# Attention with a gated layer on one core: the weights' conversion moved into PSUM, one stock of PSUM banks, and a new instruction order

## The chip, the cores and the metric

The kernel runs on one core of a Trainium2 chip. The metric is the device time of one execution, in microseconds (us). Engines are named as in the profile: PE is TensorE's matmul stream and PEld its weight loads, DVE is VectorE, ACT is ScalarE, POOL is GpSimd, SP issues the DMAs.

## The reference

There are 4 batches with 8 heads each, 1152 keys of width 64, and queries pooled in pairs to 576. Every head is softmax attention; the heads of a batch together give 576 tokens of width 512, which go through a gated layer with 1536 inner columns. The three weight matrices arrive as float64.

```python
def _attn_ref(q, k, v):
    q_pool = q.reshape(B, H, S // 2, 2, D).mean(axis=3)
    scores = np.matmul(q_pool, k.transpose(0, 1, 3, 2)) / np.sqrt(D)
    attn = np.exp(scores - np.max(scores, axis=-1, keepdims=True))
    attn = attn / (np.sum(attn, axis=-1, keepdims=True) + 1e-09)
    return np.matmul(attn, v)
def _moe_ref(x, w_gate, w_val, w_out):
    gate = 1.0 / (1.0 + np.exp(-(x @ w_gate)))
    return gate * (x @ w_val) @ w_out
```

## The kernel before, in words

The order of all instructions comes from a planner (`Plan`). Every step of the work is an `Op` with an engine, an assumed duration and a priority (a place in a sequence of heads, 18 places a head), and with the buffers that it takes and uses. `Plan.run` plays the steps through with the assumed durations and so fixes, once, the order in which each engine's instructions stand. On the chip each engine works through its own row strictly in that order and waits by semaphores; a step that comes late holds back everything behind it on its engine.

[...] The 32 heads are numbered u = 0 to 31, batch after batch:

- `head_operands` prepares a head. POOL adds the query pairs (L316). ACT writes the high halves of queries and keys (L321, L336); POOL writes their low halves (L339 for the keys, two pieces of 576 columns; L326 for some of the queries, else on DVE).
- `maxima` finds the largest score of each query: PE multiplies (L372, 384 columns), DVE reduces from PSUM (L377, L387, L389). The negated maxima are put on a diagonal in QB (L355 on POOL or DVE, L410 on POOL), so that the score product subtracts them.
- `half` does one half (288 queries) of a head: the score product into a PSUM bank (L469, two matmuls), the exponential on ACT. For the first 8 heads (`WHOLE`) one exponential and one product with the values (L486). For the others a rounded exponential eh (L473), a full one in place (L501), the difference el on DVE (L504), two products (L511, L515) and sums of eh on POOL (L533), which ACT and DVE split (L573, L576) for a last product (L580). `normalise` divides (L598 to L621).
- `convert` makes the weights usable. There are 36 pieces of 128x512 values. A piece is loaded as pairs of 32-bit words into cr (L632); ACT scales both words (L637, L642); DVE joins sign, high and low word, in place in cr (L646 `sign`, L651 `join`); ACT writes the high part (L655) and POOL the low part (L658) into cs; SP stores cs to a scratch array in DRAM (L662). The 36 pieces are spread over heads 3 to 16.
- `gated` runs the gated layer of a batch, interleaved with the attention of the next batch: 12 matmuls into one bank (L697), then ACT, DVE and POOL work (L740, L746, L750, L754), output products added up by L780 and L782. The layer of the last batch comes after all attention.

PSUM has eight banks. Before the change the planner holds them as two stocks: "b" with six for scores, value products, and gated products; "n" with two for the maxima alone:

```python
        "b": [bank[:, 512 * i:512 * i + 512] for i in range(SLOTS["b"])],
        "n": [bank[:, 512 * i:512 * i + 512] for i in range(SLOTS["b"], 8)],
```

Of the kernel before, what the change touches and what calls it, by code (L numbers as in the profile page):

```python
# [158 lines left out]
def attention_glu_kernel(ctx: ExitStack, tc: tile.TileContext, qT, kT, vt_in, v, wg, wv, wo, out):  # L159
    nc = tc.nc  # L160
    B, H, D = 4, 8, 64
    SK, SQ = 1152, 576
# [8 lines left out]
    SLOTS = {  # L171
# [3 lines left out]
    }  # L175
    pl = Plan(SLOTS, ("b", "n"))

# [25 lines left out]
    def change_first():  # L203
# [16 lines left out]
        "b": [bank[:, 512 * i:512 * i + 512] for i in range(SLOTS["b"])],  # L220
        "n": [bank[:, 512 * i:512 * i + 512] for i in range(SLOTS["b"], 8)],

# [35 lines left out]
    def tl(h):  # L258
        return TL[h.tag][h.slot]
# [8 lines left out]
    def act(n):  # L268
        return 0.01 + 0.975e-3 * n

    def dve(n):
        return 0.08 + 0.99e-3 * n

    def pool(n, two=True):
        return 0.14 + 2.2e-3 * n if two else 0.2 + 0.9e-3 * n

    def dma(kb):
        return 0.15 + kb / 250
# [14 lines left out]
    def head_operands(u, need):  # L293
# [39 lines left out]
        for k, s in enumerate((slice(0, SQ), slice(SQ, SK))):  # L333

            def k_hi(s=s):
                nc.scalar.activation(out=tl(kh)[0][:, s], in_=tl(kr)[:, s], func=ACTF.Copy)  # L336

            def k_lo(s=s):
                nc.gpsimd.tensor_tensor(out=tl(kh)[1][HI, s], in0=tl(kr)[HI, s], in1=tl(kh)[0][HI, s].bitcast(F32),  # L339
                                        op=ALU.subtract)  # L340

            a = pl.op("ACT", act(SQ), k_hi, at + 0.1 * k, after=[lk], uses=[kr] + ([kh] if k else []),
                      take=[] if k else [kh])
            ka.append(a)
            kb.append(pl.op("POOL", pool(SQ), k_lo, at + 6 + 0.1 * k, after=[a], uses=[kr, kh]))
        max_in, rest, hi_k, hi_q = [ql] + ka, [qb] + kb, ka, [qa, qb]
# [12 lines left out]
        if DGP(u):  # L359
            dg = pl.op("POOL", 2 * pool(256), lambda: diag(nc.gpsimd), need - 6, after=[am], uses=[pm, qh])  # L360
        else:
            dg = pl.op("DVE", 1.3, lambda: diag(nc.vector), need - 6, after=[am], uses=[pm, qh])
        return dict(k=kh, q=qh, v=vr, lv=lv, got=[dg] + max_in + rest, hi_k=hi_k, hi_q=hi_q)

    def maxima(at, pm, nt, lhs, rhs, out, after, uses):
        red = []
        for t in range(nt):
            for j in range(3):
                m = pl.hold("n")

# [10 lines left out]
                red.append(pl.op("DVE", dve(384), rmax, pr, after=[a], uses=[m] + ([pm] if red else []),  # L381
                                 take=[] if red else [pm], keep=KEEP))
# [65 lines left out]
    def half(u, g, st, hd, stat, vdep, pair, tk):  # L448
# [13 lines left out]
        for c in range(NC):  # L462
# [9 lines left out]
            def ex_hi(m=m, eh=eh):  # L472
# [3 lines left out]
                      uses=[hd["k"], hd["q"]], take=[m, eh])  # L476
            high = pl.op("ACT", act(GN), ex_hi, pos - 2, after=[o], uses=[m, eh])
            first = last is None
# [26 lines left out]

            o = pl.op("ACT", act(GN), ex, pos - 2, after=[high], uses=[m])
            exs.append(o)
# [32 lines left out]
        y, r = st["y"], st["r"]  # L540
        if whole:

            def cp():
                nc.scalar.activation(out=tl(y)[mine, a:b], in_=tl(av[0])[LO, 0:GN], func=ACTF.Copy)

            def cp2():
                nc.scalar.activation(out=tl(r)[mine, a:b], in_=tl(av[0])[HI, 0:GN], func=ACTF.Copy, bias=1e-9)

            ended.append(last)
            st["yo"][g].append(pl.op("ACT", act(GN), cp, at, after=[last], uses=[av[0], y]))  # L550
            st["yo"][g].append(pl.op("ACT", act(GN), cp2, at, after=[last], uses=[av[0], r]))
            return
# [74 lines left out]
    def convert(kind, m, s, due):  # L627
        src = {"wg": (wg, wv)[s], "wo": wo}[kind][m]
        cr, cs = pl.hold("cr"), pl.hold("cs")

# [37 lines left out]
        a = pl.op("DVE", 1.0, sign, due, after=[a, a0], uses=[cr])
        a = pl.op("DVE", 1.0, join, due, after=[a], uses=[cr])
        a = pl.op("ACT", act(512), hi, due, after=[a], uses=[cr], take=[cs])  # L670
        a = pl.op("POOL", pool(512), lo, due, after=[a], uses=[cr, cs])
        return pl.op("SP", dma(512), store, due, after=[a], uses=[cs], late=3.0)

# [203 lines left out]
```

## Time and profile before

| | us |
|---|---|
| median of 3 runs (964.74 to 965.56) | 965.55 |
| the profiled execution's own time | 966.0 |
| its span in the profile | 963.6 |

The profile gives for each engine the time in which an instruction of it was under way. An instruction counts from its start to its end, and on PE, ACT and DVE the next one can start before the last one has ended, so the sum of a group's durations is larger than its share of the busy time. "Idle before" is the time in which an engine had nothing under way before an instruction, with the instruction that ended the wait. Line numbers in the profile are those of the kernel before.

### The profile page before, as it was taken

To read this page: it belongs to the slowest core of one execution; us is meant where nothing else is said; L and a number is where in the kernel's file an instruction comes from. 1 tells how busy PE (TensorE), PEld (TensorE's weight loads), DVE (VectorE), ACT (ScalarE), POOL (GpSimd) and SP (SyncE) were. 2 spreads that over 40 slices of the span, in tenths; PEclk is the share of its full clock that TensorE was granted. 3 is DMA by queue.
4 is the path that set the end of the run, shared out by engine and by line. 5 is a ranking of instruction groups with operands and counts; after the bars stand their busy time and mean duration, and the time that the engine had idled before them with its cause. 6 is when DMAs were issued, how large, how long until landed. Compare 5 with 4: busy or idle time off the path is not lost.

```text
span 963.6 us, 18573 instructions
## 1 busy us (share of the span) xinstructions
PE 921.8 (96%) x6312; PEld 878.2 (91%) x6312; DVE 667.6 (69%) x1414; ACT 662.9 (69%) x1701; POOL 731.7 (76%) x796
## 2 busy tenths in 40 slices
PE   5989999999999999999999999999999999999998
PEld 3878877989998989889999999999999999999998
DVE  6576778878797998977778787877878786610112
ACT  4779788878887878677777778767777767522211
POOL 7586686988999989999988979979988967621211
PEclk9999999999999999999999999999999999999999
DMA  8687986765685848665554634544544433534532
GB/s 188 175 239 222 243 263 176 220 182 200 194 281 168 254 171 256 201 200 169 150 150 121 178 101 137 177 134 151 168 132 135 136 101 111 175 126 165 184 122 71
DMA packets 57566, 166.87 MB, mean 173 GB/s; under 512 B 17536, under 2 KB 21632, under 8 KB 51328
## 3 DMA queue, kind: packets, MB, share of 16 engines
q1 hardware_dynamic: 57472, 165.70, 56.7%
q8 instruction: 49, 0.80, 0.3%
q14 instruction: 45, 0.37, 0.1%
HBM read 132.12 MB, written 23.59 MB: 162 GB/s over the span
## 4 chain that ended last, share of the span: by engine, by line
PE 67%; POOL 10%; DVE 9%; ACT 8%; issue 3%; DMA 2%; POOLq 0%; DVEq 0%; ACTq 0%
PE bank L697 36%; PE bank L469 12%; PE bank L372 6%; PE bank L486 6%; POOL acc L533 5%; PE bank L515 4%; PE bank L511 4%; DVE cr L651 2%; DVE el L504 2%; ACT eh L473 2%; DVE pm L377 2%; ACT bank L501 1%; POOL cs L658 1%; DVE cr L646 1%; PE bank L580 1%
## 5 line engine op out<-in xcount | busy, mean ns | idle before, releaser
L697 PE MATMUL bank<-x,wg 128*128 128x288 f32 x2304 | 358.6, 296 | 2.2 <-ACT sg L740 1.1
L697 PEld LDWEIGHTS bank<-x,wg 128*128 128x128 f32 x2304 | 328.4, 188 | 4.3 <-DVE el L504 2.1
L533 POOL TENSOR_TENSOR acc<-acc,eh 128x288 f32<-128x288 f32 x312 | 261.4, 838 | 29.4 <-ACT eh L473 13.0
L504 DVE TENSOR_TENSOR el<-bank,eh 128x288 fp32r<-128x288 f32 x432 | 193.0, 452 | 86.0 <-ACT bank L501 81.6
L377 DVE TENSOR_REDUCE pm<-bank 128x1 f32<-128x384 f32 x384 | 206.6, 549 | 60.5 <-PE bank L372 58.4
L473 ACT ACTIVATE eh<-bank 128x288 fp32r<-128x288 f32 x432 | 175.9, 407 | 74.9 <-PE bank L469 69.4
L469 PE MATMUL bank<-QA,KA 128*128 128x288 f32 x576 | 172.7, 304 | 9.6 <-DVE el L504 3.2
L469 PE MATMUL bank<-QB,KB 128*128 128x288 f32 x576 | 169.1, 298 | 8.1 <-POOL QB L410 4.4
L501 ACT ACTIVATE bank<-bank 128x288 f32<-128x288 f32 x432 | 176.7, 409 | 0.1
L754 POOL TENSOR_TENSOR g<-sg,g 128x288 fp32r<-128x288 f32 x96 | 79.6, 829 | 104.6 <-ACT g L750 103.2
L372 PE MATMUL bank<-KA,QA 128*128 128x384 f32 x384 | 139.4, 377 | 12.1 <-ACT KA L336 8.5
L697 PE MATMUL bank<-g,wo 128*128 128x288 f32 x864 | 137.5, 295 | 1.0 <-ACT sg L740 0.8
L511 PE MATMUL bank<-eh,vt 128*128 128x288 f32 x432 | 128.3, 297 | 2.2 <-ACT eh L473 1.3
L515 PE MATMUL bank<-el,vt 128*128 128x288 f32 x432 | 128.6, 298 | 1.8 <-DVE el L504 1.5
L697 PEld LDWEIGHTS bank<-g,wo 128*128 128x128 f32 x864 | 124.3, 188 | 1.6 <-ACT sg L740 1.1
L469 PEld LDWEIGHTS bank<-QA,KA 128*128 128x128 f32 x576 | 109.1, 189 | 16.1 <-DVE el L504 5.4
L469 PEld LDWEIGHTS bank<-QB,KB 128*128 128x128 f32 x576 | 109.1, 189 | 10.2 <-POOL QB L410 5.5
L339 POOL TENSOR_TENSOR KB<-kr,KA 64x576 fp32r<-64x576 f32 x64 | 95.3, 1496 | 12.5 <-ACT KA L336 8.6
L746 DVE SCALAR_TENSOR_TENSOR sg<-sg,bank 128x288 f32<-128x288 f32 x96 | 43.1, 449 | 79.1 <-PE bank L697 77.6
L372 PEld LDWEIGHTS bank<-KA,QA 128*128 128x128 f32 x384 | 73.6, 192 | 25.4 <-DVE pm L377 9.6
L515 PEld LDWEIGHTS bank<-el,vt 128*128 128x128 f32 x432 | 81.5, 189 | 4.2 <-DVE el L504 3.0
L511 PEld LDWEIGHTS bank<-eh,vt 128*128 128x128 f32 x432 | 81.3, 188 | 3.7 <-ACT eh L473 2.6
(66 smaller groups left out, 1274.5 us busy)
## 6 DMA issues: line engine op xcount, KB each, us to landing
wg<-wg_d SPq DMA_DIRECT2D x48, 1024.0 KB, 5.1
kr<-in_kT_dram SPq DMA_DIRECT2D x64, 288.0 KB, 5.0
wo<-wo_d SPq DMA_DIRECT2D x36, 512.0 KB, 3.8
wg_d<-cs SPq DMA_DIRECT2D x24, 512.0 KB, 4.9
qr<-in_qT_dram SPq DMA_DIRECT2D x32, 288.0 KB, 4.0
KP<-KA SPq DMA_DIRECT2D x32, 288.0 KB, 4.1
vr<-in_v_dram SPq DMA_DIRECT2D x24, 288.0 KB, 3.0
cr<-in_wg_dram SPq DMA_DIRECT2D x12, 512.0 KB, 5.0
```

Of the source, the lines that this page charges most:

```text
L339: nc.gpsimd.tensor_tensor(out=tl(kh)[1][HI, s], in0=tl(kr)[HI, s], in1=tl(kh)[0][HI, s].bitcast(F32), op=ALU.subtract)
L372: nc.tensor.matmul(out=tl(m)[:, 0:384], lhsT=lhs(t), rhs=rhs()[:, j * 384:(j + 1) * 384], start=True, stop=True)
L377: nc.vector.tensor_reduce(out=o, in_=tl(m)[:, 0:384], axis=AXX, op=ALU.max)
L469: nc.tensor.matmul(out=tl(m)[:, 0:GN], lhsT=tl(hd["k"])[k][:, ks], rhs=tl(hd["q"])[k][:, a:b], start=(k == 0), stop=(k == 1))
L473: nc.scalar.activation(out=tl(eh), in_=tl(m)[:, 0:GN], func=ACTF.Exp, scale=1.0 / 16.0)
L501: nc.scalar.activation(out=p, in_=p, func=ACTF.Exp, scale=1.0 / 16.0)
L504: nc.vector.tensor_tensor(out=tl(el), in0=tl(m)[:, 0:GN], in1=tl(eh).bitcast(F32), op=ALU.subtract)
L511: nc.tensor.matmul(out=tl(av[0])[:, 0:GN], lhsT=pair(c, w), rhs=tl(eh), start=(c == 0), stop=(c == NC - 1))
L515: nc.tensor.matmul(out=tl(av[1])[:, 0:GN], lhsT=pair(c, 1 - w), rhs=tl(el), start=(c == 0), stop=(c == NC - 1 and not mine_c))
L533: nc.gpsimd.tensor_tensor(out=tl(acc), in0=tl(e0).bitcast(F32) if two else tl(acc), in1=tl(e1).bitcast(F32), op=ALU.add)
L697: nc.tensor.matmul(out=ps[:, 0:GN], lhsT=l, rhs=r, start=(n == 0 and j == 0), stop=(n == 3 and j == 2))
L754: nc.gpsimd.tensor_tensor(out=g[:, 1, a:b], in0=tl(sg), in1=g[:, 0, a:b].bitcast(F32), op=ALU.subtract)
```

## The change

The float64 words are no longer joined in place in SBUF. A piece now takes a PSUM bank (`wd`): ACT writes the scaled low word there, DVE's `sign` and `join` read the high word from cr and read and write the bank, ACT reads the high part from the bank, and the low part is formed by DVE instead of POOL. The two stocks of banks become one of eight, from which maxima, scores, products and conversions all take. From head 16 on, the second of the two low-half pieces of the keys is on DVE instead of POOL. The planner's assumed durations change, and with them the whole order. The count of PE instructions stays.

```diff
-        "b": 6, "n": 2, "K": 3, "Q": 3, "kr": 1, ...
+        "b": 8, "K": 3, "Q": 3, "kr": 1, ...
...
-        return 0.01 + 0.975e-3 * n
+        return 0.05 + 0.93e-3 * n
...
-        return 0.08 + 0.99e-3 * n
+        return 0.09 + 1.08e-3 * n
...
-    KEEP = 0.25
+    KEEP = 0.15
...
+    KLD = lambda u: u >= 16
...
-            def k_lo(s=s):
-                nc.gpsimd.tensor_tensor(out=tl(kh)[1][HI, s], in0=tl(kr)[HI, s], in1=tl(kh)[0][HI, s].bitcast(F32),
-                                        op=ALU.subtract)
+            by = "DVE" if k and KLD(u) else "POOL"
+
+            def k_lo(s=s, by=by):
+                e = nc.vector if by == "DVE" else nc.gpsimd
+                e.tensor_tensor(out=tl(kh)[1][HI, s], in0=tl(kr)[HI, s], in1=tl(kh)[0][HI, s].bitcast(F32),
+                                op=ALU.subtract)
...
-                m = pl.hold("n")
+                m = pl.hold("b")
...
-        cr, cs = pl.hold("cr"), pl.hold("cs")
+        cr, cs, wd = pl.hold("cr"), pl.hold("cs"), pl.hold("b")
+
+        def word():
+            return tl(wd)[:, 0:512].bitcast(U32)
...
-            low = tl(cr)[:, :, 0]
-
-            nc.scalar.activation(out=low, in_=low, func=ACTF.Copy, scale=2.0 ** -29, bias=-0.49)
+            nc.scalar.activation(out=word(), in_=tl(cr)[:, :, 0], func=ACTF.Copy, scale=2.0 ** -29, bias=-0.49)
...
-            nc.vector.scalar_tensor_tensor(out=low, in0=high, scalar=0x80000000, in1=low,
+            nc.vector.scalar_tensor_tensor(out=word(), in0=tl(cr)[:, :, 1], scalar=0x80000000, in1=word(),
...
-            nc.vector.scalar_tensor_tensor(out=low, in0=high, scalar=3, in1=low,
+            nc.vector.scalar_tensor_tensor(out=word(), in0=tl(cr)[:, :, 1], scalar=3, in1=word(),
...
-            nc.scalar.activation(out=tl(cs)[:, 0], in_=tl(cr)[:, :, 0].bitcast(F32), func=ACTF.Copy)
+            nc.scalar.activation(out=tl(cs)[:, 0], in_=tl(wd)[:, 0:512], func=ACTF.Copy)
...
-            nc.gpsimd.tensor_tensor(out=tl(cs)[:, 1], in0=tl(cr)[:, :, 0].bitcast(F32),
-                                    in1=tl(cs)[:, 0].bitcast(F32), op=ALU.subtract)
+            nc.vector.tensor_tensor(out=tl(cs)[:, 1], in0=tl(wd)[:, 0:512], in1=tl(cs)[:, 0].bitcast(F32),
+                                    op=ALU.subtract)
```

The following excerpts are the order of the built programs. In the changed file the same statements stand two to three lines lower (L649 is `sign`, L653 `join`, L660 `lo`, L507 el, L380 the maxima's reduction, L413 the small diagonal, L472 the score product).

VectorE, around the conversions at heads 9 and 10, before:

```order
L377 TENSOR_REDUCE pm_116<-bank 128x1
L576 TENSOR_TENSOR dh_104<-acc_102,dh_104 128x288
L646 SCALAR_TENSOR_TENSOR cr_142<-cr_142 128x512
L651 SCALAR_TENSOR_TENSOR cr_142<-cr_142 128x512
L504 TENSOR_TENSOR el_98<-bank,eh_94 128x288
L559 TENSOR_TENSOR y_122<-bank,t_106 64x288
```

and in the changed program:

```order
L649 SCALAR_TENSOR_TENSOR bank<-cr_141,bank 128x512
L507 TENSOR_TENSOR el_100<-bank,eh_92 128x288
L507 TENSOR_TENSOR el_101<-bank,eh_93 128x288
L562 TENSOR_TENSOR y_122<-bank,t_107 64x288
L579 TENSOR_TENSOR dh_105<-acc_103,dh_105 128x288
L507 TENSOR_TENSOR el_98<-bank,eh_94 128x288
L380 TENSOR_REDUCE pm_116<-bank 128x1
L565 TENSOR_TENSOR y_122<-bank,y_122 64x288
L507 TENSOR_TENSOR el_99<-bank,eh_95 128x288
```

The two instructions of a piece stood behind each other and behind L576; now they are apart, with el and reductions between them. The `join` of this piece follows 15 instructions after its `sign`, and its `lo` 6 after that; the piece holds its bank from ACT's write before the first of them to the last.

GpSimd, in front of the small diagonal of heads 2 and 3, before:

```order
L607 TENSOR_TENSOR y_122<-y_122,r_124 128x288
L658 TENSOR_TENSOR cs_144<-cr_143,cs_144 128x512
L621 TENSOR_TENSOR x_127<-y_122,x_127 128x288
L316 TENSOR_TENSOR qr_86<-qr_86 64x576
L658 TENSOR_TENSOR cs_145<-cr_141,cs_145 128x512
L410 TENSOR_TENSOR QB_84<-ident,pp_119 64x64
```

and in the changed program:

```order
L610 TENSOR_TENSOR y_122<-y_122,r_124 128x288
L413 TENSOR_TENSOR QB_84<-ident,pp_119 64x64
L413 TENSOR_TENSOR QB_82<-ident,pp_119 64x64
L624 TENSOR_TENSOR x_127<-y_122,x_127 128x288
L316 TENSOR_TENSOR qr_86<-qr_86 64x576
```

The two conversions are gone from POOL, and the diagonal stands ahead of the two other steps.

TensorE at the very start, before:

```order
L372 MATMUL bank<-KA_73,QA_79 128x384 x12
L469 MATMUL bank<-QA_79,KA_73 128x288
L469 MATMUL bank<-QB_82,KB_76 128x288
L372 MATMUL bank<-KA_74,QA_80 128x384 x2
L469 MATMUL bank<-QA_79,KA_73 128x288
```

and in the changed program:

```order
L375 MATMUL bank<-KA_73,QA_79 128x384 x12
L472 MATMUL bank<-QA_79,KA_73 128x288
L472 MATMUL bank<-QB_82,KB_76 128x288
L472 MATMUL bank<-QA_79,KA_73 128x288
L472 MATMUL bank<-QB_82,KB_76 128x288
```

The 12 products for the first maxima still come first, but now into eight banks instead of two, and the first scores follow without the next head's maxima between them.

## Rows read from the trace of the kernel before

**Rows 1.** The profile's page, head line.

```profile
span 963.6 us, 18573 instructions
```

**Rows 2.** Busy time by stretch: length, PE, PEld, DVE, ACT, POOL (instructions), PE clock, DMA share, GB/s.

```profile
40.00:160.00 120.00, 114.11 (x601) 97.08 (x599) 85.71 (x158) 98.19 (x237) 84.01 (x75) 1.00 0.84 234
160.00:430.00 270.00, 253.72 (x1756) 240.67 (x1755) 227.28 (x464) 216.06 (x554) 248.25 (x256) 0.99 0.66 207
430.00:840.00 410.00, 405.55 (x2951) 399.55 (x2951) 310.48 (x700) 304.14 (x816) 352.63 (x411) 1.00 0.47 143
...
350.00:400.00 50.00, 45.70 (x320) 43.16 (x320) 44.55 (x84) 39.42 (x102) 47.78 (x50) 1.00 0.70 219
```

**Rows 3.** Chain that ended last, in order of time: start, length, what (its last long piece).

```profile
839.83 120.67 PE bank L697 x909
```

**Rows 4.** Groups of 160 to 430 us on PE: count, busy and mean, idle before and releasers.

```profile
L372 PE MATMUL bank<-KA,QA 128*128 128x384 f32 x110 | 37.3, 345 | 1.6 <-DVE QA L326 1.1 <-DVE pm L377 0.4
L372 PE MATMUL bank<-KP,QP 128*128 128x384 f32 x15 | 5.5, 366 | 0.2 <-DVE pm L377 0.2
...
L469 PEld LDWEIGHTS bank<-QA,KA 128*128 128x128 f32 x162 | 30.6, 189 | 10.7 <-DVE sg L746 3.6 <-DVE el L504 3.0 <-ACT sg L740 1.8
```

**Rows 5.** Timeline near 200 us: start, length, engine, instruction, [idle before and releaser].

```profile
198.60 1.43 POOL L339 TENSOR_TENSOR KB<-kr,KA 64x576 fp32r<-64x576 f32 x1
...
199.44 0.90 DVE L576 TENSOR_TENSOR dh<-acc,dh 128x288 fp32r<-128x288 f32 x1
...
200.11 1.40 POOL L658 TENSOR_TENSOR cs<-cr,cs 128x512 fp32r<-128x512 f32 x1
...
200.27 1.79 DVE L646 SCALAR_TENSOR_TENSOR cr<-cr 128x512 uint32<-128x512 uint32 x1
...
202.09 1.17 DVE L651 SCALAR_TENSOR_TENSOR cr<-cr 128x512 uint32<-128x512 uint32 x1
...
203.18 0.44 DVE L504 TENSOR_TENSOR el<-bank,eh 128x288 fp32r<-128x288 f32 x1
...
203.68 0.40 PE L469 MATMUL bank<-QA,KA 128*128 128x288 f32 x1 [1.40 <-DVE el L504]
```

**Rows 6.** Groups of 160 to 430 us on DVE.

```profile
L504 DVE TENSOR_TENSOR el<-bank,eh 128x288 fp32r<-128x288 f32 x162 | 72.2, 450 | 24.6 <-ACT bank L501 23.8
L377 DVE TENSOR_REDUCE pm<-bank 128x1 f32<-128x384 f32 x109 | 59.0, 546 | 2.6 <-PE bank L372 2.1
L651 DVE SCALAR_TENSOR_TENSOR cr<-cr 128x512 uint32<-128x512 uint32 x20 | 24.5, 1225 | 0.2
L646 DVE SCALAR_TENSOR_TENSOR cr<-cr 128x512 uint32<-128x512 uint32 x20 | 20.6, 1031 | 1.4 <-ACT cr L637 1.4
...
L326 DVE TENSOR_TENSOR QA<-qr,QA 64x576 fp32r<-64x576 f32 x3 | 3.9, 1310 | 0.2
```

**Rows 7.** Timeline at 237 us: one of the short `sign` instructions.

```profile
236.84 0.67 DVE L646 SCALAR_TENSOR_TENSOR cr<-cr 128x512 uint32<-128x512 uint32 x1
```

**Rows 8.** Groups of 160 to 430 us on POOL: the conversions' low parts and the keys' low halves.

```profile
L339 POOL TENSOR_TENSOR KB<-kr,KA 64x576 fp32r<-64x576 f32 x18 | 28.9, 1611 | 1.2
L658 POOL TENSOR_TENSOR cs<-cr,cs 128x512 fp32r<-128x512 f32 x21 | 28.8, 1371 | 1.1 <-ACT cs L655 0.7
```

**Rows 9.** Timeline from 62 to 68 us: POOL, and the PE instruction that waited for it.

```profile
62.18 1.75 POOL L658 TENSOR_TENSOR cs<-cr,cs 128x512 fp32r<-128x512 f32 x1
...
66.00 1.28 POOL L658 TENSOR_TENSOR cs<-cr,cs 128x512 fp32r<-128x512 f32 x1
67.25 0.65 POOL L410 TENSOR_TENSOR QB<-ident,pp 64x64 fp32r<-64x64 f32 x2
...
67.59 0.40 PE L469 MATMUL bank<-QB,KB 128*128 128x288 f32 x1 [2.34 <-POOL QB L410]
```

**Rows 10.** Groups of 40 to 160 us on PE: the second matmul of the score products.

```profile
L469 PE MATMUL bank<-QB,KB 128*128 128x288 f32 x126 | 35.5, 299 | 5.4 <-POOL QB L410 4.4 <-POOL QB L355 1.0
```

**Rows 11.** Timeline of the start: a pair of reductions, the first diagonal, the first full score product.

```profile
14.62 1.13 DVE L377 TENSOR_REDUCE pm<-bank 128x1 f32<-128x384 f32 x2 [0.21 <-PE bank L372]
...
17.32 1.97 DVE L355 TENSOR_TENSOR QB<-ident,pm 64x256 fp32r<-64x256 f32 x2
...
19.44 0.58 PE L469 MATMUL bank<-QB,KB 128*128 128x288 f32 x1 [2.71 <-DVE QB L355]
```

More of the change, by code (lines that the diff above doesn't have):

```diff
@@ L175, in attention_glu_kernel @@
     }
-    pl = Plan(SLOTS, ("b", "n"))
+    pl = Plan(SLOTS, ("b",))
     const = ctx.enter_context(tc.tile_pool(name="const", bufs=1))
@@ L220, in attention_glu_kernel @@
         "b": [bank[:, 512 * i:512 * i + 512] for i in range(SLOTS["b"])],
-        "n": [bank[:, 512 * i:512 * i + 512] for i in range(SLOTS["b"], 8)],
         "K": list(zip(SK_T("KA"), SK_T("KB"))),
@@ L344, in head_operands @@
             ka.append(a)
-            kb.append(pl.op("POOL", pool(SQ), k_lo, at + 6 + 0.1 * k, after=[a], uses=[kr, kh]))
+            kb.append(pl.op(by, pool(SQ) if by == "POOL" else 1.0, k_lo, at + 6 + 0.1 * k, after=[a], uses=[kr, kh]))
         max_in, rest, hi_k, hi_q = [ql] + ka, [qb] + kb, ka, [qa, qb]
@@ L359, in head_operands @@
         if DGP(u):
-            dg = pl.op("POOL", 2 * pool(256), lambda: diag(nc.gpsimd), need - 6, after=[am], uses=[pm, qh])
+            dg = pl.op("POOL", 1.5, lambda: diag(nc.gpsimd), need - 6, after=[am], uses=[pm, qh])
         else:
@@ L380, in maxima @@
                 a = pl.op("PE", pe(384), mm, pr, after=after, uses=uses, take=[m])
-                red.append(pl.op("DVE", dve(384), rmax, pr, after=[a], uses=[m] + ([pm] if red else []),
+                red.append(pl.op("DVE", 0.49, rmax, pr, after=[a], uses=[m] + ([pm] if red else []),
                                  take=[] if red else [pm], keep=KEEP))
@@ L476, in half @@
                       uses=[hd["k"], hd["q"]], take=[m, eh])
-            high = pl.op("ACT", act(GN), ex_hi, pos - 2, after=[o], uses=[m, eh])
+            high = pl.op("ACT", 0.3, ex_hi, pos - 2, after=[o], uses=[m, eh])
             first = last is None
@@ L504, in lo @@
                 nc.vector.tensor_tensor(out=tl(el), in0=tl(m)[:, 0:GN], in1=tl(eh).bitcast(F32), op=ALU.subtract)
-            o = pl.op("ACT", act(GN), ex, pos - 2, after=[high], uses=[m])
+            o = pl.op("ACT", 0.345, ex, pos - 2, after=[high], uses=[m])
             exs.append(o)
@@ L536, in half @@
                     two = len(adds) == 2
-                    added = pl.op("POOL", pool(GN), add, pos + 0.5, after=[high, added, adds[0][1]],
+                    added = pl.op("POOL", 0.88, add, pos + 0.5, after=[high, added, adds[0][1]],
                                   uses=[eh] + ([adds[0][0]] if two else [acc]), take=[acc] if two else [])
@@ L550, in half @@
             st["yo"][g].append(pl.op("ACT", act(GN), cp, at, after=[last], uses=[av[0], y]))
-            st["yo"][g].append(pl.op("ACT", act(GN), cp2, at, after=[last], uses=[av[0], r]))
+            st["yo"][g].append(pl.op("ACT", 0.42, cp2, at, after=[last], uses=[av[0], r]))
             return
@@ L565, in cp2 @@
             nc.scalar.activation(out=tl(r)[mine, a:b], in_=tl(av[1])[other, 0:GN], func=ACTF.Copy, bias=1e-9)
-        o = pl.op("ACT", act(GN), cp3, at, after=[last], uses=[av[0]], take=[th])
-        part = pl.op("DVE", dve(GN), plus, at, after=[o], uses=[av[0], th, y])
+        o = pl.op("ACT", 0.42, cp3, at, after=[last], uses=[av[0]], take=[th])
+        part = pl.op("DVE", 0.46, plus, at, after=[o], uses=[av[0], th, y])
         if mine_c:
@@ L582, in half @@
             o = pl.op("ACT", act(GN), acc_hi, at, after=[added], uses=[acc], take=[dh])
-            o = pl.op("DVE", 0.6, acc_lo, at, after=[o], uses=[acc, dh])
+            o = pl.op("DVE", 0.72, acc_lo, at, after=[o], uses=[acc, dh])
             last = pl.op("PE", 2 * pe(GN), den, at + 2, after=[o, last], uses=[dh, av[1]])
-        st["yo"][g].append(pl.op("DVE", dve(GN), plus2, at + 1, after=[part, last], uses=[av[1], y]))
-        st["yo"][g].append(pl.op("ACT", act(GN), cp2, at + 1, after=[last], uses=[av[1], r]))
+        st["yo"][g].append(pl.op("DVE", 0.46, plus2, at + 1, after=[part, last], uses=[av[1], y]))
+        st["yo"][g].append(pl.op("ACT", 0.42, cp2, at + 1, after=[last], uses=[av[1], r]))
     def normalise(p, g, st):
@@ L607, in mult @@
             nc.gpsimd.tensor_tensor(out=y, in0=y, in1=tl(st["r"])[:, a:b], op=ALU.mult)
-        nm = pl.op("DVE", 1.16 if NMP(p) else 1.6, norm, s, after=st["yo"][g], uses=[st["y"], st["r"]], take=[th])
+        nm = pl.op("DVE", 1.2 if NMP(p) else 1.65, norm, s, after=st["yo"][g], uses=[st["y"], st["r"]], take=[th])
         if NMP(p):
@@ L665, in convert @@
         gate.append((a, min(max(0, int(due) - AHEAD), LAST_GATE)))
-        a0 = pl.op("ACT", act(512), low_bits, due, after=[a], uses=[cr])
+        a0 = pl.op("ACT", act(512), low_bits, due, after=[a], uses=[cr], take=[wd])
         a = pl.op("ACT", act(512), scale, due, after=[a], uses=[cr])
[L668 to L671, printed above, removed]
+        a = pl.op("DVE", dve(512), sign, due, after=[a, a0], uses=[cr, wd])
+        a = pl.op("DVE", dve(512), join, due, after=[a], uses=[cr, wd])
+        a = pl.op("ACT", act(512), hi, due, after=[a], uses=[wd], take=[cs])
+        a = pl.op("DVE", dve(512), lo, due, after=[a], uses=[wd, cs])
         return pl.op("SP", dma(512), store, due, after=[a], uses=[cs], late=3.0)
```

6 lines of the change are left out of this document (2 added, 4 removed), and 2 rows, old and new, of the table SLOTS.

## The prediction

> **What bounds the kernel now.** Of the span of 963.6 us [rows 1] I read the busy time by stretch first. PE is the fullest engine in every stretch [rows 2], so the question is where PE, whose work the change leaves as it is, loses time. The last stretch gives its undisturbed pace: 909 matmuls of 288 columns in 120.67 us, 0.1328 us each [rows 3]. From 160 to 430 us PE carried out 1756 matmuls [rows 2], of which 125 have 384 columns [rows 4]; at the same pace per column (0.177 us) they and the 1631 others need 22.1 + 216.6 = 238.7 us. The stretch lasts 270, so 31 us are lost there. This is where the first batch's gated layer, the second batch's attention and 20 or 21 of the 36 conversions run together. From 430 to 840 us PE is idle for only 4.5 of 410 us, from 40 to 160 us for 5.9 of 120 [rows 2]; the tail is PE alone [rows 3].
>
> What holds PE in the long stretch? POOL is busy for 248.3 of 270 us (92%), DVE for 227.3 (84%), ACT for 216.1 (80%) [rows 2]. Yet PE hardly waits for POOL directly: the weight loads of the score products stand idle for 10.7 us, until DVE or ACT has freed a bank [rows 4]. The timeline near 200 us shows how. DVE has three instructions in a row with both inputs in SBUF, 0.90, 1.79 and 1.17 us long, while POOL works on keys and a conversion; the el behind them starts at 203.18, and PE, which needs the bank of an el, stands for 1.40 us [rows 5]. On average `sign` takes 1.03 here and `join` 1.23 [rows 6]; one `sign` elsewhere takes 0.67 [rows 7]. So POOL's fullness is mostly paid on DVE: the two lengthen each other.
>
> **The change part by part.** The sum is made against the profiled execution, 966.0 us (its span and 2.4 us around it), which is 0.45 above the median of the runs.
>
> *Conversions, 160 to 430 us.* POOL loses 21 instructions of 1.37 us, 28.8 us in all [rows 8]. DVE loses 24.5 + 20.6 us [rows 6] and gains three instructions a piece, about 61 of 512 columns with one input in PSUM and one in SBUF. Two of them write PSUM, which no DVE instruction of this trace does. From below, 0.68 us: el has the same kinds of input and takes 0.450 for 288 columns, the reduction 0.546 for 384, so a column costs 0.0010 and 512 columns 0.45 + 0.224 = 0.68; the short `sign` at 0.67 agrees [rows 6, 7]. From above, 1.13, the mean of today's two. I take 0.68, the row with the same kinds of input, whose mean of 0.450 shows no stretching though POOL is busy for 92% of the time. That is 61 x 0.68 = 41.5 us. The keys' pieces of heads 16 and 17 add 2 x 1.31 = 2.6 us on DVE (the like subtraction for the queries costs that here) and take 3.2 from POOL [rows 6, 8]. ACT keeps its three instructions a piece; costed at nothing, since it has 54 us idle. So DVE needs 227.3 - 45.1 + 41.5 + 2.6 = 226.3 us, POOL 216, ACT 216, PE 239. DVE is now the fullest behind PE. If its share stays at 84.2%, the stretch lasts 269 us, a gain of 1. In its fullest 50 us it reaches 44.55, a share of 0.891, with POOL still fuller beside it [rows 2], so that is no ceiling of its own; at 0.891 the stretch lasts 254. If PE idles there as little as from 430 to 840 us (1.1%), it lasts 242. I take 254, since that row is the nearest to a DVE-bound stretch: a gain of **16**, ends 1 and 28.
>
> [...] Measured, the PSUM input costs next to nothing: 0.68 from the el against 0.67 for two SBUF inputs [rows 6, 7]. [...] No run yet shows such an instruction at 512 columns.
>
> *Conversions, 40 to 160 us.* The other 15 or 16 pieces. POOL and DVE have slack; what counts is the small diagonal behind them. At 62 us two conversions (1.75 and 1.28) stand in front of it, and PE waits 2.34 [rows 9]; such waits sum to 5.4 us [rows 10]. The changed order has no conversion there and the diagonal ahead of two other steps. I take **2.5**, the wait that the rows show, ends 0 and 5.4.
>
> *One stock of banks, start.* The first 12 products go to two banks, and each pair of reductions is followed by 0.2 us of waiting for PE, six times: 1.2 us. ACT now writes the keys' high part ahead of QB's, 0.7 earlier. PE waits 2.71 us for the diagonal behind the reductions [rows 11]. I take **1.5**, ends 0 and 2.7.
>
> *Keys on DVE, 430 to 840 us.* 14 pieces of some 1.31 us go to DVE, 18.3 us on 310.5 of 410; POOL loses as many of 1.6. The cover is DVE's idle 99 us. If it is gone: from 160 to 430 us, 45.1 us of long DVE instructions went with 16.3 us of idle PE, 0.36 a us, which makes 6.6 us of loss. Above stands all of PE's idle time here, 4.5. With POOL at 86% [rows 2] losing 22 us and maxima no longer confined to two banks, I take a gain of **1**.
>
> The tail: nothing. Sum: 16 + 2.5 + 1.5 + 1 = 21 us; 966.0 - 21 = 945.0, and against the median **944.5 us**.
>
> **The rivals.**
>
> *Banks become short (959).* A converting piece holds its bank over some 20 DVE instructions, at half a us each about 10 us; 21 pieces hold 210 bank-us of the 254, 0.8 of a bank. Against it: the 125 products for maxima [rows 4], at perhaps 1 us of hold, fill only half a bank of the two that were theirs, so 1.5 come free. If the holds are twice as long, nothing comes free, PE waits for banks as before, and the stretch gains only its lower end, 1: 966 - 1 - 5 = 960, against the median 959.
>
> *VectorE becomes the bound, slower (975).* If the three instructions cost what today's two do, 1.13 us, DVE needs 184.8 + 61 x 1.13 = 253.7 us, at a share of 0.891 that is 285, 15 more than now; less the 5 gained elsewhere, 10 more. It decides from 0.92 us an instruction on, where 184.8 + 61 x 0.92 = 0.891 x 270. For it: POOL still reads SBUF most of the time. Against it: el, also with one SBUF input, stays at 0.450 [rows 6]. [...]
>
> *Everything opens (932.5).* The stretch falls to 242, a gain of 28 instead of 16. For it: POOL, DVE and ACT would all be at 89 to 94%. Against it: that is fuller than DVE and ACT are in any row here.
>
> **How the numbers follow.** Forecast 0.68, banks 0.15, VectorE 0.08, everything 0.07; 0.02 is left for an order that loses as much as it wins. A measurement of this kernel tells 0.2%, 1.9 us, from no change. The forecast's own range goes from 936 to 953 (the stretch gains 24 to 8). The given range, **933 to 960**, adds the banks' case and most of everything, and leaves out VectorE and the tails. Faster: 0.68 + 0.07 and nearly all of the banks' case, 0.89; same 0.03; slower 0.08.
>
> **What would show it.** After the change `sign`, `join` and `lo` should last 0.65 to 0.75 us each, also beside POOL; POOL should lose some 75 us of busy time (36 pieces of 1.37 and 16 of 1.61), with none left on conversions; the waits for POOL's small diagonal should be gone; and PE's 1756 matmuls from 160 us on should take about 254 us, with DVE at about 0.89. Wrong would be: these three near 1 us; PE waiting for banks that conversions hold (their releasers would be the readers of `wd`); or a stretch of 270 us with POOL at 80%, which would mean that POOL was never what held it.

## The result, and the profile after

The changed kernel takes 936.71 us (median of 4 runs, 935.87 to 937.78), the kernel before 965.47 beside it (964.74 to 965.56). The ratio is 0.9704 (95% interval 0.9688 to 0.9721): 28.8 us less, where 21 were forecast. One execution of 1263.67 us, at a granted clock of 0.659, is left out of a median below (the planner's figures alone). The head of the page of the profile after answers to [rows 1]:

```profile
span 935.0 us, 18634 instructions
...
PE 910.1 (97%) x6312; PEld 878.3 (94%) x6312; DVE 679.3 (73%) x1466; ACT 658.5 (70%) x1701; POOL 645.6 (69%) x744
```

To see where the 28.8 us came from, the two traces are cut where PE has done the same work (each matmul counted with its undisturbed pace: 0.1328 us for 288 columns, 0.177 for 384, 0.243 for the value products of the first heads). The cuts lie near those of the prediction, at 39.8, 160.3, 432.2 and 840.9 us of before, and are good to about half a us. A gain of 1 us between two neighbouring stages hangs on where the cut lies: with one at 430.0, the gains of the long stretch and of the later one are 18.4 and 5.1 in place of 19.8 and 3.7.

| us | start | first heads | long stretch | later | tail |
|---|---|---|---|---|---|
| before | 39.8 | 120.5 | 271.9 | 408.7 | 122.7 |
| after | 34.7 | 120.5 | 252.1 | 405.0 | 122.7 |
| gain measured | 5.1 | 0.0 | 19.8 | 3.7 | 0.0 |
| gain forecast | 1.5 | 2.5 | 16 | 1 | 0 |

Busy time by stretch of the kernel after answers to [rows 2], with the same columns (length, PE, PEld, DVE, ACT, POOL, granted clock, DMA share, GB/s):

```profile
160.00:414.00 254.00, 250.73 (x1798) 245.25 (x1798) 224.92 (x482) 212.16 (x555) 203.27 (x233) 0.99 0.69 215
414.00:812.00 398.00, 394.56 (x2900) 392.11 (x2900) 317.50 (x699) 297.24 (x799) 330.61 (x391) 1.00 0.47 143
...
34.70:155.20 120.50, 118.10 (x603) 98.40 (x602) 90.48 (x181) 102.89 (x249) 61.73 (x63) 1.00 0.89 261
155.00:408.00 253.00, 248.42 (x1767) 241.30 (x1766) 224.60 (x483) 212.38 (x551) 202.75 (x232) 0.99 0.70 216
```

In the long stretch PE is now busy for 98% of the time, where it was 94%. POOL went from 92% to 80%. DVE stands at 224.92 of 254, a share of 0.886, almost the 0.89 that was forecast.

The groups on DVE from 160 to 408 us answer to [rows 6] (count, busy and mean, idle before):

```profile
L507 DVE TENSOR_TENSOR el<-bank,eh 128x288 fp32r<-128x288 f32 x162 | 72.4, 452 | 12.3 <-ACT bank L504 10.8
...
L660 DVE TENSOR_TENSOR cs<-bank,cs 128x512 fp32r<-128x512 f32 x19 | 12.9, 685 | 0.5
L653 DVE SCALAR_TENSOR_TENSOR bank<-cr,bank 128x512 uint32<-128x512 uint32 x17 | 11.7, 687 | 0.1
...
L649 DVE SCALAR_TENSOR_TENSOR bank<-cr,bank 128x512 uint32<-128x512 uint32 x17 | 11.7, 685 | 0.2
...
L342 DVE TENSOR_TENSOR KB<-kr,KA 64x576 fp32r<-64x576 f32 x3 | 3.2, 1052 | 0.1
```

`sign` (L649), `join` (L653) and `lo` (L660) last 0.685 to 0.687 us; the first two were 1.031 and 1.225. There are 17 pieces in the stretch now where there were 20: three have moved to the first heads, which gain nothing, so the two stages are best read together (19.8 measured, 18.5 forecast). The weight loads of the score products, idle for 10.7 us in [rows 4], are at 3.2:

```profile
L472 PEld LDWEIGHTS bank<-QA,KA 128*128 128x128 f32 x164 | 31.0, 189 | 3.2 <-DVE y L562 1.0 <-DVE el L507 0.7 <-ACT r L568 0.5
```

The timeline of the start answers to [rows 11]:

```profile
9.05 5.78 DVE L380 TENSOR_REDUCE pm<-bank 128x1 f32<-128x384 f32 x12 [1.23 <-PE bank L375]
...
15.06 0.85 DVE L358 TENSOR_TENSOR QB<-ident,pm 64x256 fp32r<-64x256 f32 x2
...
15.77 1.41 POOL L326 TENSOR_TENSOR QA<-qr,QA 64x576 fp32r<-64x576 f32 x1 [0.79 <-ACT QA L321]
...
16.06 0.58 PE L472 MATMUL bank<-QB,KB 128*128 128x288 f32 x1 [3.04 <-DVE QB L358]
```

and in the kernel before POOL worked beside the diagonal of 17.32:

```profile
17.58 2.98 POOL L339 TENSOR_TENSOR KB<-kr,KA 64x576 fp32r<-64x576 f32 x2 [0.48 <-ACT KA L336]
```

With eight banks the twelve reductions run back to back, 0.48 us each, in 5.78 us instead of six pairs of 1.13 + 0.21, which is 8.0. The diagonal takes 0.85 instead of 1.97: POOL's next instruction that reads SBUF starts at 15.77 now, when the diagonal is nearly done; before the change one started 0.26 us after the diagonal began. The first full score product starts at 16.06 instead of 19.44.

The waits for POOL's diagonals [rows 10] are gone, but PE is not earlier at the end of the first heads. The weight loads from 35 to 155 us wait for ACT in their place. The first row is of before (40 to 160 us), the others are of after:

```profile
L469 PEld LDWEIGHTS bank<-QA,KA 128*128 128x128 f32 x126 | 23.7, 188 | 0.5
...
L489 PEld LDWEIGHTS bank<-e,ve 128*128 128x128 f32 x255 | 46.7, 189 | 11.5 <-ACT e L476 1.4
...
L472 PEld LDWEIGHTS bank<-QA,KA 128*128 128x128 f32 x125 | 23.5, 188 | 6.0 <-ACT e L476 2.9 <-ACT r L550 1.2
L375 PEld LDWEIGHTS bank<-KA,QA 128*128 128x128 f32 x85 | 15.9, 188 | 3.1 <-ACT e L476 1.4 <-ACT r L550 0.4 <-POOL QB L358 0.3
```

### The profile page after: what moved, and what is told of

It reads as the page before. It is cut to its first block, busy times and chain, and to the rows that moved or that the text cites. A ratio compares the mean times of both kernels' runs of the same rounds, so it can differ in the third digit from the quotient of the medians.

```text
span 935.0 us, 18634 instructions
## 1 busy us (share of the span) xinstructions
PE 910.1 (97%) x6312; PEld 878.3 (94%) x6312; DVE 679.3 (73%) x1466; ACT 658.5 (70%) x1701; POOL 645.6 (69%) x744
## 4 chain that ended last, share of the span: by engine, by line
PE 86%; DVE 8%; ACT 4%; issue 1%; DMA 1%; POOL 0%; SPq 0%; ACTq 0%; POOLq 0%; DVEq 0%
PE bank L699 45%; PE bank L472 15%; PE bank L375 7%; PE bank L489 7%; PE bank L518 6%; PE bank L514 5%; DVE pm L380 2%; DVE dh L579 2%; PE bank L583 1%; DVE el L507 1%; DVE pp L380 1%; DMA kr<-in_kT_dram 1%; ACT e L476 1%; ACT eh L476 1%; POOL acc L536 0%
## 5 line engine op out<-in xcount | busy, mean ns | idle before, releaser
L536 POOL TENSOR_TENSOR acc<-acc,eh 128x288 f32<-128x288 f32 x312 | 258.4, 828 | 52.6 <-ACT eh L476 37.2
L380 DVE TENSOR_REDUCE pm<-bank 128x1 f32<-128x384 f32 x384 | 204.8, 551 | 58.5 <-PE bank L375 54.3
L507 DVE TENSOR_TENSOR el<-bank,eh 128x288 fp32r<-128x288 f32 x432 | 192.9, 452 | 54.1 <-ACT bank L504 49.8
L472 PE MATMUL bank<-QA,KA 128*128 128x288 f32 x576 | 177.7, 311 | 2.6 <-ACT e L476 1.3
L472 PE MATMUL bank<-QB,KB 128*128 128x288 f32 x576 | 169.2, 297 | 3.0 <-DVE QB L358 3.0
L375 PE MATMUL bank<-KA,QA 128*128 128x384 f32 x384 | 131.9, 357 | 9.3 <-ACT KA L336 8.3
L472 PEld LDWEIGHTS bank<-QA,KA 128*128 128x128 f32 x576 | 109.3, 190 | 9.7 <-ACT e L476 2.9
L472 PEld LDWEIGHTS bank<-QB,KB 128*128 128x128 f32 x576 | 109.3, 190 | 4.9 <-issue 3.4
L742 ACT ACTIVATE sg<-bank 128x288 f32<-128x288 f32 x96 | 39.3, 409 | 56.7 <-PE bank L699 56.1
```

What stands on the lines that cost most here:

```text
L472: nc.tensor.matmul(out=tl(m)[:, 0:GN], lhsT=tl(hd["k"])[k][:, ks], rhs=tl(hd["q"])[k][:, a:b], start=(k == 0), stop=(k == 1))
L507: nc.vector.tensor_tensor(out=tl(el), in0=tl(m)[:, 0:GN], in1=tl(eh).bitcast(F32), op=ALU.subtract)
```

## The experiments

The theory that came out of the prediction: the conversions' long DVE instructions, stretched beside POOL, hold PE in the long stretch; short, they leave DVE's share (0.89) as the bound. The rivals: banks are short; DVE, now fuller, is what costs; POOL's relief alone is the gain; or it is only the new order. Ratios are against the kernel before, run beside each kernel: 965.28 us for the first four, 964.54 for the next four, 964.96 for the last three. Stages are given in the order of the table. Every kernel is planned anew and so has its own order: even the POOL instruction added in the last experiment puts a matmul of another kind in 650 of PE's 6312 places. A difference of a few us can therefore be the order's alone. First the three parts, each alone in the kernel before, and the new conversion with its words in SBUF.

**Conversion alone.** Only `convert` of after, in the kernel before:

```diff
-        cr, cs = pl.hold("cr"), pl.hold("cs")
+        cr, cs, wd = pl.hold("cr"), pl.hold("cs"), pl.hold("b")
...
-        a = pl.op("POOL", pool(512), lo, due, after=[a], uses=[cr, cs])
+        a = pl.op("DVE", dve(512), lo, due, after=[a], uses=[wd, cs])
```

> The kernel before with only the conversion changed (word in a bank of the six, low part on DVE; two stocks, old figures, keys on POOL). If the conversion carries the gain of the stretch from 160 us on, about 950 us (15 of the 16 forecast, nothing at the start). If the new order or the bank stock carries it, 960 or more, since then the shorter DVE instructions only turn into waiting elsewhere. If two maxima banks and a word in the six make banks short, 962 to 970, with PE waiting for bank releases for more than the 10.7 us of before.

955.31 us, ratio 0.9894 (0.9879 to 0.9908). The stages: 39.4, 118.6, 265.3, 408.3, 122.5. The time lies between the cases that were expected. POOL is relieved and the three instructions are short, yet the long stretch gains only 6.6 us. The groups on PEld (first row) and DVE from 160 to 425 us:

```profile
L469 PEld LDWEIGHTS bank<-QA,KA 128*128 128x128 f32 x162 | 30.4, 188 | 10.8 <-DVE el L504 5.1 <-ACT sg L739 1.3 <-DVE cs L657 1.3
```

```profile
L650 DVE SCALAR_TENSOR_TENSOR bank<-cr,bank 128x512 uint32<-128x512 uint32 x20 | 13.7, 687 | 0.2
L646 DVE SCALAR_TENSOR_TENSOR bank<-cr,bank 128x512 uint32<-128x512 uint32 x20 | 13.7, 686 | 1.8 <-ACT cr L640 1.3 <-ACT bank L643 0.3
```

The idle time ahead of the score products is what it was, 10.8 against 10.7 [rows 4], and 1.3 of it now ends with `lo` (cs L657), which frees the word's bank. That the six banks are a seat short is only argued from this; the kernel with two stocks below tests it.

**Banks alone.** One stock of eight in the kernel before:

```diff
-        "b": 6, "n": 2, "K": 3, "Q": 3, ...
+        "b": 8, "K": 3, "Q": 3, ...
...
-                m = pl.hold("n")
+                m = pl.hold("b")
```

> The kernel before with only one stock of eight banks. The start should gain 4 to 5 us, as in the changed kernel, whose first score product came 3.4 us earlier; the stretch with the conversions should stay, since DVE and POOL keep their loads: 960 to 962 us. If banks are what held PE between 160 and 430 us, 950 or less.

955.01 us, 0.9894 (0.9879 to 0.9909); stages 34.7, 117.6, 269.6, 408.3, 122.6. That is 5 us better than expected, since the next two stages gain 2.9 and 2.3 as well. The whole gain at the start, 5.1, is the banks'. In the timeline the reductions are as short as in after, and the diagonal is still long, with POOL's L325 reading SBUF beside it:

```profile
8.94 5.77 DVE L376 TENSOR_REDUCE pm<-bank 128x1 f32<-128x384 f32 x12 [1.41 <-PE bank L371]
...
14.95 1.96 DVE L354 TENSOR_TENSOR QB<-ident,pm 64x256 fp32r<-64x256 f32 x2
15.23 1.40 POOL L325 TENSOR_TENSOR QA<-qr,QA 64x576 fp32r<-64x576 f32 x1 [0.79 <-ACT QA L320]
```

So the shorter diagonal of after is not what the stage's length hangs on.

**Planner's figures alone.** All new durations and KEEP in the kernel before, nothing else:

```diff
-        return 0.14 + 2.2e-3 * n if two else 0.2 + 0.9e-3 * n
+        return 0.18 + 2.35e-3 * n if two else 0.2 + 0.9e-3 * n
...
-    KEEP = 0.25
+    KEEP = 0.15
```

> The kernel before with only the planner's new assumed durations, and so a new order of the same instructions. If the gain is a matter of work and ports, 962 to 968 us. If the order itself carries it, 950 or less.

952.2 us, 0.9865 (0.9848 to 0.9881); stages 39.4, 119.0, 265.4, 404.0, 123.4. No operation changed, only the order, and it is worth 13.1 us alone, 4.7 of them in the later stretch.

**Word in SBUF, `lo` on DVE.** The changed kernel, but the word stays in cr, so that POOL is relieved as in after while all three instructions have both inputs in SBUF:

```diff
-            nc.vector.scalar_tensor_tensor(out=word(), in0=tl(cr)[:, :, 1], scalar=3, in1=word(),
+            nc.vector.scalar_tensor_tensor(out=low, in0=high, scalar=3, in1=low,
...
-            nc.vector.tensor_tensor(out=tl(cs)[:, 1], in0=tl(wd)[:, 0:512], in1=tl(cs)[:, 0].bitcast(F32),
+            nc.vector.tensor_tensor(out=tl(cs)[:, 1], in0=tl(cr)[:, :, 0].bitcast(F32),
```

> The changed kernel with the word joined in place in SBUF again and the low part still on DVE: POOL is as free as in the changed kernel, but each of the three DVE instructions has both inputs in SBUF. If POOL's time is what counted, it stays at 936 to 941 us. If the DVE instructions beside POOL count, they last about 1.0 us each instead of 0.685, 108 x 0.3 = 34 us more on DVE, 20 of them in the long stretch, which then lasts 20 / 0.89 = 22 us longer: 955 to 962 us.

957.81 us, 0.9928 (0.9907 to 0.995); stages 34.2, 114.4, 279.8, 406.4, 122.6. The long stretch is 27.7 longer than in after and 7.9 longer than before, with POOL at 210.05 of 270 us. The window of the stretch, the DVE groups from 160 to 425 us, and the timeline near 160 us:

```profile
160.00:430.00 270.00, 252.15 (x1722) 242.27 (x1723) 240.37 (x474) 211.14 (x535) 210.05 (x221) 0.96 0.70 211
```

```profile
L654 DVE SCALAR_TENSOR_TENSOR cr<-cr 128x512 uint32<-128x512 uint32 x21 | 23.4, 1116 | 0.2
L649 DVE SCALAR_TENSOR_TENSOR cr<-cr 128x512 uint32<-128x512 uint32 x21 | 21.9, 1042 | 0.0
L661 DVE TENSOR_TENSOR cs<-cr,cs 128x512 fp32r<-128x512 f32 x21 | 21.2, 1008 | 2.0 <-ACT cs L658 2.0
```

```profile
157.00 1.32 DVE L661 TENSOR_TENSOR cs<-cr,cs 128x512 fp32r<-128x512 f32 x1
158.25 1.88 DVE L649 SCALAR_TENSOR_TENSOR cr<-cr 128x512 uint32<-128x512 uint32 x1
160.17 1.17 DVE L654 SCALAR_TENSOR_TENSOR cr<-cr 128x512 uint32<-128x512 uint32 x1
161.25 0.54 DVE L380 TENSOR_REDUCE pm<-bank 128x1 f32<-128x384 f32 x1
...
161.85 1.09 PE L700 MATMUL bank<-x,wg 128*128 128x288 f32 x3 [3.78 <-DVE pm L380]
```

Three long instructions in a row stand ahead of a reduction for 4.25 us, and PE stands for 3.78 us waiting for its bank: the picture of [rows 5], enlarged. What follows on PE is a lower granted clock, 0.50 and then 0.85 (windows of the same trace):

```profile
150.00:160.00 10.00, 7.21 (x41) 5.60 (x39) 9.36 (x18) 9.93 (x27) 8.50 (x12) 0.98 0.11 32
160.00:165.00 5.00, 3.15 (x13) 3.15 (x14) 4.97 (x10) 3.01 (x5) 4.36 (x3) 0.50 0.67 238
165.00:170.00 5.00, 5.00 (x35) 5.00 (x34) 2.35 (x8) 3.75 (x10) 2.82 (x5) 0.85 0.99 255
```

So relieving POOL alone is not the gain: without the short form of the three instructions the stretch is longer than before. This kernel does not tell whether the short form counts by the length of each instruction or by DVE's whole time, since both grew: DVE is busy for 240.37 of 270 us, a share of 0.890, and over the same PE work for 250.1 us where it is 224.0 in after.

Next, what each part is worth in the changed kernel.

**Old conversion in the changed kernel.** `convert` of before, `lo` on POOL again; all else as after:

```diff
-        a = pl.op("DVE", dve(512), lo, due, after=[a], uses=[wd, cs])
+        a = pl.op("POOL", pool(512), lo, due, after=[a], uses=[cr, cs])
```

> The changed kernel with the conversion of before (in place in SBUF, low part on GpSimd); one stock, new figures and keys on DVE stay. If the parts add up as they did alone (8 to 10 us for the conversion), 945 to 947 us, the longer part of it between 160 and 430 us. If the conversion is worth its forecast 16 to 18 us only once order and banks let it through, 952 to 956.

944.99 us, 0.9795 (0.9781 to 0.981); stages 34.2, 114.9, 263.9, 404.0, 124.3. The conversion is worth 11.8 us in the long stretch and costs 5.6 in the first heads; as 20 pieces lie in the long stretch here and 17 in after, part of both is pieces that moved.

**Keys on POOL.** The keys' low halves go back to POOL:

```diff
-    KLD = lambda u: u >= 16
+    KLD = lambda u: False
```

> The changed kernel with all the keys' low halves on GpSimd. If the keys' move gives the gain after 430 us (3.7 us there), 940 to 941 us, with that stretch at 408. If it is the new order (it was 4.7 without the move when the figures were changed alone), 936 to 938.

932.75 us, 0.9675 (0.9651 to 0.9699); stages 34.2, 119.6, 249.8, 403.6, 122.9. That is below both cases that were expected: this part of the change costs some 4 us by the medians, 2.8 by the ratios. The intervals of this kernel and of after (0.9688 to 0.9721) overlap a little, so it is the best version measured, but not by a safe distance. The two orders are the same up to 321 us, and at 332 us both traces have PE at the same matmul; the difference opens behind. In the first two stages, in the same order, they still differ by 0.5 and 0.9: so much is the noise of one execution and of the cuts. On DVE a key piece, which has two SBUF inputs, takes 1.052 us (L342 above).

**Two stocks.** Six and two banks in the changed kernel:

```diff
-        "b": 8, "K": 3, "Q": 3, ...
+        "b": 6, "n": 2, "K": 3, "Q": 3, ...
```

> The changed kernel with six banks and two again; the word takes one of the six. The start should lose its 5 us. If banks matter to the conversions too, the rest loses 5 or more as well: 946 to 952 us. If one stock helps the start alone, 941 to 943.

957.71 us, 0.9928 (0.9912 to 0.9945); stages 38.0, 120.0, 266.7, 407.8, 123.2. This is worse than either case expected. The PEld group of the score products from 160 to 410 us, idle for 8.8 us where it is 3.2 in after:

```profile
L473 PEld LDWEIGHTS bank<-QA,KA 128*128 128x128 f32 x151 | 28.3, 188 | 8.8 <-DVE el L508 3.8 <-DVE sg L749 1.6 <-DVE cs L661 0.9
```

The common stock is worth 21.0 us here and 10.3 alone. Where the word takes no bank it is worth less here too: the kernels with the figures alone (952.2) and with the old conversion (944.99) differ by the stock and the keys' move, and by 7.2 us. What the stock adds is the seat for the word.

**Old figures.** The changed kernel with the planner's durations and KEEP of before:

```diff
-    KEEP = 0.15
+    KEEP = 0.25
```

> The changed kernel planned with the old assumed durations. If the parts add up, the figures are worth 11 to 13 us: 947 to 950 us, lost between 160 and 430 us (6) and after (4 to 5). If the conversion and the banks alone make the gain, 936 to 940.

941.01 us, 0.9754 (0.974 to 0.9769); stages 33.8, 117.6, 255.0, 409.2, 122.5. On top of the rest the figures are worth 4.3 us, and 4.2 of that lies in the later stretch.

Then the first heads, and the two causes still mixed in the long stretch.

**Early pieces in SBUF.** Keys on POOL, and the pieces due early converted as before, the others through PSUM:

```diff
-  stored[kind, m_] = [convert(kind, m_, s, due) for s in range(2 if k < 4 else 1)]
+  stored[kind, m_] = [(convert_sbuf if due < 140 else convert)(kind, m_, s, due) for s in range(2 if k < 4 else 1)]
```

> The version with all keys' halves on GpSimd (932.8 us), with the pieces due before place 140 converted in SBUF as before and the rest through PSUM. If the word's bank and the extra DVE instruction slow the stretch of the first 8 heads (120 us with the word in a bank, 114 to 115 in the two runs without), it gains 5: 927 to 929 us. If the number of pieces taken early is the cause (19 against 16), no more than 1 to 2 us change: 931 to 934.

935.16 us, 0.9696 (0.9681 to 0.9712); stages 36.1, 115.8, 252.6, 407.4, 123.1. The first heads gain 3.8 on the kernel with the keys on POOL, and the other stages give back more, so that neither expected time came. Of the 16 pieces in the first heads here 12 are converted in SBUF; number and form changed together.

**`sign` twice.** A second `sign` behind the first, which leaves the word as it is: 36 more DVE instructions, all short.

```diff
         a = pl.op("DVE", dve(512), sign, due, after=[a, a0], uses=[cr, wd])
+        a = pl.op("DVE", dve(512), sign, due, after=[a], uses=[cr, wd])
```

> The changed kernel with each piece's sign instruction given twice (the second one changes nothing): 36 x 0.69 us more on DVE, some 17 of them in the long stretch. If DVE's time sets that stretch, 17 x 0.69 / 0.885 = 13 us more: 948 to 952 us. If banks or PE itself set it, under 5 more: 937 to 942.

940.29 us, 0.975 (0.9733 to 0.9767); stages 34.7, 120.0, 255.5, 405.0, 123.3. Windows, to be held against the rows of after:

```profile
155.00:408.00 253.00, 247.69 (x1743) 237.65 (x1742) 230.68 (x497) 210.85 (x546) 199.73 (x229) 1.00 0.69 214
```

18 of them fall into the long stretch, 18 x 0.69 = 12.4 us by their durations (DVE's busy time over the same PE work grows by 8.7, from 224.0 to 232.8). The stretch grows by 3.4. DVE goes to 230.68 of 253, a share of 0.912. So 0.89 was no bound: DVE worked more when it was given more.

**POOL busy again.** A POOL instruction per piece, of about the size of the old `lo`, reading SBUF; its result is not used:

```diff
+            nc.gpsimd.tensor_tensor(out=tl(cr)[:, :, 0].bitcast(F32), in0=high, in1=high, op=ALU.subtract)
```

> The changed kernel with one GpSimd subtraction of 512 columns a piece, whose result nobody reads: POOL gets back the time that the conversion took from it (36 x 1.3 us), DVE keeps its one SBUF input. If POOL's time is what held PE, 946 to 950 us. If DVE's instructions are, 936 to 940.

936.62 us, 0.9707 (0.9692 to 0.9722); stages 34.2, 119.6, 251.7, 405.4, 123.8. The window of the long stretch, the group of the added POOL instruction in it, and those of DVE's `sign` and `join` beside it:

```profile
155.00:408.00 253.00, 248.24 (x1769) 240.48 (x1770) 221.86 (x482) 212.41 (x552) 219.80 (x249) 1.00 0.69 212
```

```profile
L654 POOL TENSOR_TENSOR cr<-cr 128x512 f32<-128x512 f32 x17 | 18.2, 1075 | 0.0
```

```profile
L649 DVE SCALAR_TENSOR_TENSOR bank<-cr,bank 128x512 uint32<-128x512 uint32 x17 | 11.7, 686 | 0.1
L657 DVE SCALAR_TENSOR_TENSOR bank<-cr,bank 128x512 uint32<-128x512 uint32 x17 | 11.6, 685 | 0.1
```

With 18 us of POOL work back, `sign` and `join` keep their 0.685 and the time is that of after. Beside short DVE instructions, POOL's relief brought nothing, as far as this kernel goes: POOL is at 87%, where it was at 92% before, and nothing waits for the added instruction.

## Why the prediction was right, and where not

The time lies in the range, 7.8 us below the forecast. It came nearer than the stages did: they miss by 3.6, -2.5, 3.8 and 2.7 us, which in part cancel. Point by point:

- **The 0.68 us.** Right: 0.685 to 0.687 in place of 1.031 and 1.225, also with POOL at 219.8 of 253 us. With the word in SBUF the same three take 1.01 to 1.12 us. From PSUM `sign` takes 0.685, 0.015 us more than the short one from SBUF, 0.67 [rows 7]. Of the prediction's own working, 0.45 + 0.224 is 0.674 and 238.7 / 0.989 is 241, roundings that move under half a us of the forecast.
- **The long stretch, 16.** Measured 19.8, and the picture foretold came (252 us, DVE at 0.886). Yet the step that turned DVE's time into PE's, that the stretch is as long as DVE's busy time over a share of 0.891, failed. With `sign` twice the stretch should then have grown by 10 to 14 us (8.7 or 12.4, over 0.891); it grew by 3.4 at a share of 0.912. Nor can DVE's total have made the gain: over the same PE work it only fell from 229.2 to 224.0 us. [rows 5] and the word in SBUF show single waits of PE behind trains of long DVE instructions, with a lower clock after some (0.66 behind [rows 5], 0.50 with the word in SBUF). They are not shown to be the whole: in the trace of before, PE stands idle for 17.5 us of the stretch, and its pauses of 0.3 us and more in which a DVE instruction of over 0.8 us ran make 6.9 of them (1.2 of 4.6 in after, 13.8 of 20.6 with the word in SBUF). What the rest of the lost time hung on stays open; the new order and the common stock, each alone, take 6.5 and 2.3 us from the stretch. That DVE came out near 0.89 was luck: PE itself is busy for 98% of the stretch now.
- **Banks become short.** The rival is true of the change without the common stock: 957.71 with two stocks, where 959 was given. The one stock averts it. The hold was put too low: from ACT's write to the end of `lo` a piece holds its bank for 14.2 us on average in the trace of after (10 estimated), which makes 1.24 banks over the stretch instead of 0.8. That is still less than the 1.5 that were to come free, a figure that no run measured.
- **VectorE becomes the bound, slower.** Its condition (0.92 us or more each) is met with the word in SBUF. The long stretch became 279.8 against its 285, and 250.1 us of DVE time at its share of 0.891 would be 281, so there its rule holds; with `sign` twice it does not. The whole stayed faster than before by the start (5.6 us), the first heads (6.1) and the later stretch (2.3).
- **40 to 160 us, 2.5.** Failed: 0. The waits for the diagonals fell as forecast, but 19 pieces are now converted there instead of 16, ACT is at 102.89 of 120.5 us, and PE waits for ACT. The step that failed is that a removed wait is a gain, without asking what is late next. Two kernels with the whole word in SBUF took 114.4 and 114.9 there, with 15 and 16 pieces, and the one with early pieces in SBUF 115.8 with 16. Whether the number of pieces or their form costs more is not settled: 16 pieces went through PSUM in 117.6 with the old figures, and in 118.6 with the conversion alone.
- **Start, 1.5.** Mis-sized: 5.1, all of it with the banks alone. Only the pauses between pairs were counted (1.2 us); the reductions, once fed without a break, follow each other every 0.48 us instead of every 0.67 (half of 1.13 + 0.21), and all that stands behind them moves up.
- **430 to 840 us, 1 from the keys on DVE.** The cause was wrong. The gain of 3.7 is the order's (4.7 with the figures alone, nothing with the old figures), and moving the keys brought none: by the two traces it costs 1.4 there and 2.3 in the long stretch, little above the noise of a stage.
- **POOL's 75 us and the tail.** 731.7 to 645.6, a loss of 86; the tail is unchanged at 122.7.

Taken away one at a time, the conversion is worth 8.3 us by the medians, the common stock 21.0, the figures 4.3 and the keys' move -4.0, which is 29.6 together; by the ratios it is 8.8, 21.6, 4.8 and -2.8, 32.4 together. Alone the first three bring 10.0, 10.3 and 13.1. They overlap, so no such sum has to give the 28.8 measured, and the stock and the conversion need each other.

## What to carry to other kernels

Ask of a shared engine not only how full it is but how long the longest train of its instructions is that stands between the fullest engine and its next buffer; 12.4 us more of short instructions on a full engine cost 3.4 here. Scratch in PSUM made them short here (0.685 to 0.687 us in place of 1.031 and 1.225), and paid off in full only where the banks were pooled (936.71 us, against 957.71 with two stocks), so that the scratch took none from the matmuls. And when a planner's figures change along with the work, test them by themselves: here a new order alone was worth more than either real change alone (13.1 us, against 10.0 and 10.3).

## What the runs showed of the hardware that was not expected

Behind some waits of PE its granted clock was lower, so that such a wait went with a loss beyond its length. With the word in SBUF PE stood for 3.78 us up to 161.85, and the granted clock was 0.50 from 160 to 165 us and 0.85 in the next five. There are four such places in the stretch (0.68, 0.83, 0.83 and 0.77 over 10 us each). That the wait brings the lower clock is concluded from their order alone, and it does not follow every wait: from 310 to 320 us PE is idle for 2.29 us at a clock of 1.00. The mean clock from 160 to 430 us is 0.96 there, against 0.99 or 1.00 in all other kernels. By an estimate from these, 0.04 of 270 is 11 us lost to the clock, up to 3 are lost in after (0.01 of 254, a rounded figure), so that about 8 of the 27.7 us are the clock and the rest the waits and DVE's added work. In the kernel before there is one such place, behind the waits of [rows 5] (windows near 205 us):

```profile
200.00:205.00 5.00, 3.46 (x22) 2.71 (x20) 4.84 (x8) 2.22 (x6) 4.77 (x5) 1.00 0.35 126
205.00:210.00 5.00, 4.28 (x21) 4.27 (x21) 3.19 (x8) 2.61 (x9) 2.87 (x4) 0.66 0.58 165
```

ACT also gained from PSUM, which no term had: writing the word to a bank took 0.632 us and reading it 0.596, where the same steps in SBUF took 0.672 and 0.669 before (two rows of after, then two of before):

```profile
L646 ACT ACTIVATE bank<-cr 128x512 uint32<-128x512 uint32 x17 | 10.7, 632 | 0.0
L657 ACT ACTIVATE cs<-bank 128x512 fp32r<-128x512 f32 x17 | 10.1, 596 | 0.7 <-DVE bank L653 0.5
...
L655 ACT ACTIVATE cs<-cr 128x512 fp32r<-128x512 f32 x21 | 14.1, 669 | 4.2 <-DVE cr L651 4.2
...
L642 ACT ACTIVATE cr<-cr 128x512 uint32<-128x512 uint32 x20 | 13.4, 672 | 0.1
```
